# A fused attention and two-layer block kernel: one of its products computed from seven block products in place of eight

## The chip, the core and the metric

The kernel runs on one core of a Trainium2 chip. The core has a tensor engine (PE, with its weight loads shown apart as PEld), a vector engine (DVE), a scalar engine (ACT), a general engine (POOL) and SP, which here issues the DMAs. SBUF is the on-chip memory; PSUM is the memory into which PE writes. The metric is the device time of one execution in microseconds (us).

## What is computed

Four batches of 576 tokens. First a masked attention with 8 heads of 64, then a mixing layer, then a gated layer:

```python
def _moe_ref(x, mu_k, mu_r, w_k, w_v, w_r):
    x_prev = np.concatenate([np.zeros((B, 1, D)), x[:, :-1, :]], axis=1)
    xk = mu_k * x + (1.0 - mu_k) * x_prev
    xr = mu_r * x + (1.0 - mu_r) * x_prev
    k = np.maximum(xk @ w_k, 0.0)             # 512 -> 1024
    v = k * k @ w_v                           # 1024 -> 512
    r = 1.0 / (1.0 + np.exp(-(xr @ w_r)))     # 512 -> 512
    return r * v
def _moe2_ref(x, w_in, w_spatial, b_spatial, w_out):
    h = np.maximum(x @ w_in, 0.0)             # 512 -> 1024
    u, v = h[..., :512], h[..., 512:]
    v_n = (v - mean(v)) / sqrt(var(v) + 1e-6)
    v_s = einsum('ts,bsd->btd', w_spatial, v_n) + b_spatial
    return (u * v_s) @ w_out
```

The product that the change touches is `xr @ w_r` of the last batch.

## The kernel before

Channels lie on partitions in blocks of 128 (the 512 channels are 4 blocks), tokens along the free dimension. The mixing layer works on a batch in two halves of 288 tokens. A matrix number is held as a high and a low part, and a product is the sum of three matmuls of 128x128 by 128x288: high by high, high by low, low by high. They add up in one PSUM bank per output block; three banks `psM` (names psM_93, psM_94, psM_102) serve these products in turn.

For each batch b and half hf, `moe1_k` (line 1472) makes k with 8 output blocks of 4 inputs, and its square with high and low parts (`sq_dt`, on ACT, DVE and POOL); `moe1_r` (line 1539) makes r with 4 output blocks of 4 inputs and writes the Tanh of each from PSUM into `xs[b]` on ACT; `moe1_v` (line 1559) makes v with 4 output blocks of 8 inputs, and a DVE instruction (`gate`, line 1567) multiplies it into `xs[b]` from PSUM, which frees the bank. After that the second layer takes `xs[b]`: vt, u (from seven block products for batches 1 to 3, `fast_u`, line 1877), sp and out. Its PSUM banks `psB` are in the room that the attention's banks had.

Weights come as pairs of 32-bit words. `split_weight` (line 646) takes one by chunks of 128x512: a load of 512 KB into one of two buffers `raw2` issued by SP, two passes on ACT (`tmp<-raw`, `raw<-raw`), one on DVE (`lower`, line 705: `tmp<-tmp,raw`) after which the buffer can be loaded again, then the high part (a cast, ACT or DVE) and the low part (a subtraction, DVE or POOL). w_in has 8 such chunks, w_out 4; w_out's high and low parts go into the room of w_r (`square_`), which must be done with. The w_spatial loads follow through the same two buffers; PE transposes them.

The two buffers and w_in's parts lie in the SBUF pool "w2", which takes the place of the attention's pool "att" at the right side of SBUF. `open_w2` (line 1669) opens it when all users of the attention's keys are done:

```python
    def open_w2(e):
        stacks["att"].close()
        enter("two", "w2", side="right", reuse_waits="tile")
    ...
    plan.at = 4905
    add({}, open_w2, w=["w2"], after=users_of(att_keys), lat=0)
```

The order of all instructions on all engines is set before the program runs: every step is put on a list (`Plan`, line 191) with its estimated time on each engine that can do it, the keys it reads and writes, and a place `plan.at`; a list scheduler takes the steps by priorities, which a table `TUNE` of numbers shifts by tag, and picks the engine. The instructions are then issued in that order through a helper (line 497, so the profile shows L497 for all), and are kept in it.

## Time and profile before

| | us |
|---|---|
| three runs | 570.43, 573.19, 573.49 |
| median | 573.19 |
| profiled execution | 570.87 |
| its span, first to last instruction | 569.1 |
| PE busy in the span | 558.2 (98%) |
| DVE, ACT, POOL busy | 361.8, 263.9, 143.3 |
| mean granted TensorE clock | 0.999 |

The profiled execution is one of its own; 1.8 us of its time lie outside the span. A name such as `psM<-xh,wk` is output and inputs; buffer numbers are left out. Idle time of an engine is put down to what ended it.

### The profile page before, as it was taken

What the parts mean: (1) busy time and instruction counts of PE and PEld (TensorE: products, weight loads), DVE (VectorE), ACT (ScalarE), POOL (GpSimd) and SP (SyncE); (2) the same over time, 40 slices, a digit from 0 to 9 for tenths busy, and PEclk for the clock granted to TensorE, in tenths of its full rate; (3) what the DMA queues carried; (4) which work ended last, traced back from release to release, by engine and by line L of the source; (5) the groups of instructions that cost most, each with busy time, mean ns of one, the idle gap of its engine ahead of it and who ended that gap; (6) DMA issues with size and microseconds to landing.
All of it is one profiled execution on the core that took longest, in us unless ns stands there. A gap on an engine that the chain in (4) does not pass through costs nothing.

```text
span 569.1 us, 13965 instructions
## 1 busy us (share of the span) xinstructions
PE 558.2 (98%) x5810; PEld 504.7 (89%) x5821; DVE 361.8 (64%) x808; ACT 263.9 (46%) x599; POOL 143.3 (25%) x159
## 2 busy tenths in 40 slices
PE   8899999999999999999999999999999999999997
PEld 5567878799999999999999999989879988998996
DVE  3789889667976485466816245575598438857740
ACT  2779874451763552568936151263253234203131
POOL 0011201450233441313112026016411712104040
PEclk9999999999999999999999999999999999999999
DMA  8999972560461041333400001300010010001002
GB/s 191 251 239 262 235 169 44 131 123 11 90 126 49 2 86 38 96 111 132 134 32 2 1 1 46 79 2 2 37 38 1 0 56 37 1 1 74 2 1 93
DMA packets 86688, 43.10 MB, mean 76 GB/s; under 512 B 71968, under 2 KB 79648, under 8 KB 86624
## 3 DMA queue, kind: packets, MB, share of 16 engines
q1 hardware_dynamic: 86624, 42.21, 30.7%
q8 instruction: 45, 0.74, 0.6%
q14 instruction: 19, 0.16, 0.1%
HBM read 37.47 MB, written 4.72 MB: 74 GB/s over the span
## 4 chain that ended last, share of the span: by engine, by line
PE 89%; SPq 4%; ACT 2%; DVE 2%; DMA 2%; issue 1%; DVEq 0%; ACTq 0%
PE psM L497 64%; PE psB L497 18%; PE psT L497 5%; SPq L497 4%; PE psS L497 2%; DMA vw<-in_v_dram 1%; DMA ld<-in_k_dram 0%; ACT xh L497 0%; DVE temps L497 0%; DVE st L497 0%; DVE xm L497 0%; ACT vw L497 0%; DVE wk L497 0%; ACT tmp L497 0%; ACT room L497 0%
## 5 line engine op out<-in xcount | busy, mean ns | idle before, releaser
L497 PE MATMUL psM<-sq_dt.float32r,wv 128*128 128x288 f32 (+2 forms) x768 | 113.0, 297 | 0.4 <-ACT x L497 0.2
L497 PEld LDWEIGHTS psM<-sq_dt.float32r,wv 128*128 128x128 f32 x768 | 104.6, 188 | 2.4 <-ACT x L497 0.9
L497 PE MATMUL psM<-xh,wk 128*128 128x288 f32 (+2 forms) x320 | 92.7, 341 | 0.0
L497 PE MATMUL psM<-xh,square 128*128 128x288 f32 (+2 forms) x256 | 64.4, 309 | 0.6 <-ACT kr L497 0.6
L497 PEld LDWEIGHTS psM<-xh,wk 128*128 128x128 f32 x320 | 58.4, 188 | 5.2 <-DVE pr L497 0.5
L497 PE MATMUL psM<-xh,lasting 128*128 128x288 f32 x192 | 57.8, 301 | 0.0
L497 PE MATMUL psM<-xl,lasting 128*128 128x288 f32 x192 | 56.4, 294 | 0.0
L497 ACT ACTIVATE kr<-psM 128x288 f32<-128x288 f32 (+2 forms) x59 | 24.1, 411 | 57.7 <-PE psM L497 54.4
L497 PEld LDWEIGHTS psM<-xh,square 128*128 128x128 f32 x256 | 44.5, 188 | 2.6 <-ACT kr L497 1.6
L497 PE MATMUL psB<-wi,lasting 128*128 128x512 f32 x176 | 45.6, 395 | 0.0
L497 POOL TENSOR_TENSOR sq_dt.float32r<-kr,sq_dt.float32r 128x288 fp32r<-128x288 f32 (+2 forms) x29 | 24.3, 839 | 64.7 <-DVE sq_dt.float32r L497 51.0
L497 PE MATMUL psB<-square,gh 128*128 128x512 f32 (+1 forms) x136 | 40.4, 381 | 0.0
L497 PEld LDWEIGHTS psB<-wi,lasting 128*128 128x128 f32 x176 | 32.3, 188 | 6.9
L497 PE MATMUL psM<-wsh,vh 128*128 128x288 f32 x128 | 38.1, 298 | 0.0
L497 PE MATMUL psM<-xl,square 128*128 128x288 f32 (+2 forms) x128 | 37.9, 296 | 0.0
L497 PE MATMUL psM<-wsh,vl 128*128 128x288 f32 x128 | 37.8, 295 | 0.0
L497 PE MATMUL psM<-wsl,vh 128*128 128x288 f32 x128 | 37.8, 295 | 0.0
L497 PEld LDWEIGHTS psM<-xh,lasting 128*128 128x128 f32 x192 | 36.0, 188 | 0.6 <-DVE x L497 0.2
L497 PEld LDWEIGHTS psM<-xl,lasting 128*128 128x128 f32 x192 | 36.0, 188 | 0.0
L497 DVE CAST sq_dt.float32r<-kr 128x288 fp32r<-128x288 f32 (+2 forms) x38 | 11.8, 310 | 37.2 <-ACT kr L497 37.2
L497 DVE SCALAR_TENSOR_TENSOR xm<-x,mu,xm 128x288 f32<-128x288 f32 (+2 forms) x56 | 30.5, 557 | 7.0 <-ACT xm L497 6.5
L497 DVE TENSOR_TENSOR g<-psM,bb 128x288 f32<-128x288 f32 x32 | 14.5, 456 | 31.7 <-PE psM L497 25.1
(199 smaller groups left out, 1237.3 us busy)
## 6 DMA issues: line engine op xcount, KB each, us to landing
vw<-in_v_dram SPq DMA_DIRECT2D x36, 128.0 KB, 3.1
room<-in_moe_w_k_dram SPq DMA_DIRECT2D x8, 512.0 KB, 9.0
room<-in_moe_w_v_dram SPq DMA_DIRECT2D x8, 512.0 KB, 7.6
raw<-in_moe_w_in_dram SPq DMA_DIRECT2D x8, 512.0 KB, 3.9
vw<-in_v_dram SPq DMA_DIRECT2D x8, 288.0 KB, 5.8
ld<-in_q_dram SPq DMA_DIRECT2D x32, 72.0 KB, 2.7
ld<-in_k_dram SPq DMA_DIRECT2D x32, 72.0 KB, 2.6
room<-in_moe_w_r_dram SPq DMA_DIRECT2D x4, 512.0 KB, 5.7
```

The costliest lines, as they stand in the source:

```text
L497: return self.tc.keep_in_program_order(getattr(self.engine, name)(*args, **kw))
```

## The change

r of batch 3 (both halves at once) is no longer made by `moe1_r`. The matrix product is cut in blocks: the 512 inputs into two halves, the 512 outputs into two halves, the 576 tokens into two halves. Eight block products make it in the plain way; here seven do (Strassen, in Winograd's form), on sums of weight blocks (`sumh`, `suml`) and of token blocks (`tokh`, `tokl`). `open_rs` closes the attention's pool, opens a pool "rs" in its place, and makes the weight sums; `moe1_r7` mixes the tokens into `mixed`, makes their parts and sums, and adds the seven products up in place in `mixed` (2 copies and 14 additions); `moe1_r7_gate` writes the Tanh of each into `xs[3]`. The pool "w2" now takes the place of "rs", so `open_w2` waits for all steps of these functions. All numbers in `TUNE` are replaced, which changes the order and the choice of engines in many places.

```diff
--- before.py
+++ after.py
 TUNE = {
...
-    ('r', 3, 0): {'g': (5327, -33735, 792, 22), 'psM': (-6229, -150948, 792, 22), 'xh': (-8333, 200588, 200, 22), 'xl': (-5995, 87640, 0, 300), 'xm': (-5709, 229219, 792, 22)},
-    ('r', 3, 1): {'g': (-5636, -92591, 792, 22), 'psM': (-4640, 98437, 792, 22), 'xh': (-5279, -52865, 792, 22), 'xl': (-5431, -79038, -600, 0), 'xm': (-7328, -219772, 400, 22)},
+    ('r7', 3): {'g': (-7563, -43040, 792, 22), 'psM': (-6469, 1566, 792, 22), 'rc': (1719, -9997, 792, 22)},
+    ('rT', 3): {'rTh': (-2631, 10737, 792, 22), 'rTl': (-8567, 5537, 0, 300), 'rmix': (-1886, 16678, -200, -300), 'rpart': (-7239, -787, -600, -800)},
+    ('rs sums',): {'rS': (-4347, -9753, 1500, 2000), 'rst': (-6149, 34735, -600, 2000), 'rsy': (72, -12010, -600, 22)},
...
+    SEVEN = (3,)
+    QW = DM // 2
+    rs_ops = set()
+    def rs(shape, dtype, name):
+        return lambda: get("rs", shape, dtype, name)
+    mixed_all = rs([P, NC, S], F32, "mixed")
...
+    made_keys = set()
+    def open_rs():
+        att_keys = [
+            key for key in plan.written
+            if key == "mask" or isinstance(key, tuple)
+            and key[0] in ("ld", "vw", "qT", "kT", "pr", "mx", "sm", "pt", "psS", "psT")
+        ]
+        def emit(e):
+            stacks["att"].close()
+            enter("rs", "rs", side="right", reuse_waits="tile")
+            enter("two", "psB", space=PSUM, reuse_waits="tile")
+        plan.at = 4900
+        plan.tag = ("rs room",)
+        add({}, emit, w=["rs"], after=users_of(att_keys), lat=0)
...
+        for j in range(2):
+            plan.at = 5000 + 20 * j
+            parts = []
+            for y in range(2):
+                o = lambda y=y: flat()[:, y * CH : (y + 1) * CH]
+                key = ("wr", j + 2 * y, 0)
+                add(
+                    {"pool": pool(CH), "dve": dve(CH)},
+                    lambda e, o=o, key=key: two(e, o(), f32(chunk(key, 0)), f32(chunk(key, 1)), ALU.add),
+                    r=["rs", (key, 0), (key, 1)], w=[("rsy", y)], two=True,
+                )
+                parts.append([lambda o=o, z=z: o()[:, z * QW : (z + 1) * QW] for z in range(2)])
...
+            for i, x, y, op in (
+                (0, a21, a22, ALU.add), (1, lo[0], a11, ALU.subtract), (2, a11, a21, ALU.subtract),
+                (3, a12, lo[1], ALU.subtract),
+            ):
...
+                add(
+                    {"pool": pool(QW), "dve": dve(QW)},
+                    lambda e, i=i, x=x, y=y, op=op, lo=lo: two(e, lo[i](), x(), y(), op),
+                    r=[("rsy", 0), ("rsy", 1)] + dep, w=[("rst", i)], two=True,
+                )
...
+            add(
+                {"act": act(4 * QW), "dve": dve2(4 * QW)},
+                lambda e, j=j, st=st: copy(e, sum_h()[:, j], st()),
+                r=los, w=[("rS", j, 0)], two="both",
+            )
+            add(
+                {"pool": pool(4 * QW), "dve": dve(4 * QW)},
+                lambda e, j=j, st=st: two(e, sum_l()[:, j], st(), f32(sum_h()[:, j]), ALU.subtract),
+                r=los + [("rS", j, 0)], w=[("rS", j, 1)], two=True,
+            )
...
+    def product7(m, ps, key, wof, xof):
+        for j in range(2):
+            def emit(e, j=j):
+                wh, wl = wof[0](j, m)
+                rh, rl = xof[0](j)
+                o_ = ps[:, :HALF]
+                nc.tensor.matmul(o_, wh, rh, start=j == 0, stop=False)
+                nc.tensor.matmul(o_, wh, rl, start=False, stop=False)
+                nc.tensor.matmul(o_, wl, rh, start=False, stop=j == 1)
+            add(
+                {"pe": pe(3, HALF)}, emit,
+                r=wof[1](j) + xof[1](j) + ([key] if j else []), w=[key], lat=200 if j else 0,
+            )
+    def moe1_r7(b, base):
+        plan.at = base
+        plan.tag = ("rm", b)
...
+        for c in range(NC):
+            mk = ("rmix", c)
+            made_keys.add(mk)
+            def before_(e, c=c):
...
+            add(
+                {"act": act(S), "dve": dve2(S)}, before_,
+                r=["rs", ("rest", 1), *xkeys(b, 0, c)], w=[mk], two="both", after=free,
+            )
+            add(
+                {"dve": 130 + S * 1.042},
+                lambda e, c=c: nc.vector.scalar_tensor_tensor(
+                    mixed_all()[:, c], xs[b][:, c, 1 : 1 + S], mu[:, 1, c : c + 1], mixed_all()[:, c],
+                    op0=ALU.mult, op1=ALU.add,
+                ),
+                r=[mk, ("mu", 1), *xkeys(b, 0, c)], w=[mk], two=True,
+            )
...
+        plan.tag = ("rT", b)
...
+        for i, o, p, q_, dep in (
+            (0, t0, lambda: x(0, 1), lambda: x(0, 0), []),
+            (2, t2_, lambda: x(1, 1), lambda: x(0, 1), []),
+            (1, t0, lambda: x(1, 1), t0, []),
+            (3, t0, lambda: x(1, 0), t0, []),
+        ):
...
+            add(
+                {"pool": pool(2 * HALF), "dve": dve(2 * HALF)},
+                lambda e, o=o, p=p, q_=q_: two(e, o(), p(), q_(), ALU.subtract),
+                r=own + ([tk] if i in (1, 3) else []), w=[tk], two=True, after=before_t2,
+            )
+            add(
+                {"act": act(2 * HALF), "dve": dve2(2 * HALF)},
+                lambda e, i=i, o=o: copy(e, tok_h()[:, i], o()), r=[tk], w=[("rTh", i)], two="both",
+            )
+            add(
+                {"pool": pool(2 * HALF), "dve": dve(2 * HALF)},
+                lambda e, i=i, o=o: two(e, tok_l()[:, i], o(), f32(tok_h()[:, i]), ALU.subtract),
+                r=[tk, ("rTh", i)], w=[("rTl", i)], two=True,
+            )
+        plan.tag = ("r7", b)
+        gone = users_of(own + [("rmix", "t2")])
...
+        for m in range(2):
+            def place(ff, th, m=m):
+                return lambda: mixed_all()[:, 2 * ff + m, th * HALF : (th + 1) * HALF]
...
+            plan.at = base + 100 + 100 * m
+            pa, ka = bank()
+            product7(m, pa, ka, W(0, 0), X[0, 0])
+            add(
+                {"act": actp(HALF), "dve": dve(HALF)},
+                lambda e, ps=pa, o=place(1, 0): copy(e, o(), ps[:, :HALF]),
+                r=[ka], w=[key_of(1, 0)], after=gone,
+            )
+            for w, x_, adds in (
+                (W(2, 0), X[1, 0], [((0, 0), (1, 0))]),
+                (SW(1), TX(1), [((0, 1), (1, 0))]),
+                (SW(2), TX(2), [((1, 1), (0, 1))]),
+                (W(2, 1), TX(3), [((1, 0), (1, 1))]),
+                (SW(0), TX(0), [((1, 1), (1, 1)), ((0, 1), (0, 1))]),
+                (SW(3), X[1, 1], [((0, 1), (0, 1))]),
+            ):
+                plan.at += 15
+                ps, key = bank()
+                product7(m, ps, key, w, x_)
+                for o, i in adds:
+                    add(
+                        {"dve": dve(HALF)},
+                        lambda e, o=place(*o), i=place(*i), ps=ps: two(e, o(), ps[:, :HALF], i(), ALU.add),
+                        r=[key, key_of(*i)], w=[key_of(*o)], after=gone,
+                    )
...
+    def moe1_r7_gate(b, hf):
+        plan.tag = ("r7", b)
+        for o in range(NC):
+            users = set()
+            for xk in xkeys(b, 1, o):
+                users |= plan.read[xk]
+            add(
+                {"act": act(HALF)},
+                lambda e, o=o: nc.scalar.activation(
+                    xs[b][:, o, hf * HALF : (hf + 1) * HALF],
+                    mixed_all()[:, o, hf * HALF : (hf + 1) * HALF], AF.Tanh, scale=0.5,
+                ),
+                r=[("rc", o, hf)], w=[("g", b, o, hf)], table="exp", after=users,
+            )
...
+        if b == min(SEVEN):
+            n0 = len(plan.ops)
+            open_rs()
+            rs_ops.update(range(n0, len(plan.ops)))
         for hf in range(2):
             base = 1000 * (2 * b + hf + 1)
             plan.at = base
             kk = moe1_k(b, hf)
             plan.at = base + r_at[2 * b + hf]
-            moe1_r(b, hf)
+            if b in SEVEN:
+                n0 = len(plan.ops)
+                if hf == 0:
+                    moe1_r7(b, plan.at)
+                plan.at = base + r_at[2 * b + hf]
+                moe1_r7_gate(b, hf)
+                rs_ops.update(range(n0, len(plan.ops)))
+            else:
+                moe1_r(b, hf)
...
-    att_keys = [
-        key for key in plan.written
-        if key == "mask" or isinstance(key, tuple) and key[0] in ("ld", "vw", "qT", "kT", "pr", "mx", "sm", "pt", "psS", "psT")
-    ]
-
     def open_w2(e):
-        stacks["att"].close()
+        stacks["rs"].close()
         enter("two", "w2", side="right", reuse_waits="tile")
-        enter("two", "psB", space=PSUM, reuse_waits="tile")
 
...
     plan.at = 4905
     plan.tag = ("p2",)
-    add({}, open_w2, w=["w2"], after=users_of(att_keys), lat=0)
+    add({}, open_w2, w=["w2"], after=set(rs_ops), lat=0)
```

On PE, the end of r(3,0) in before and of r in after. `xh,square` and `xl,square` are tokens by w_r, `sumh` and `suml` weight sums, `wv` is v. Before:

```order
L497 MATMUL psM_94<-xh_1_887,square 128x288
L497 MATMUL psM_94<-xh_1_914,square 128x288
L497 MATMUL psM_94<-xl_928,square 128x288
L497 MATMUL psM_94<-xh_1_914,square 128x288
L497 MATMUL psM_102<-sq_dt.float32r,wv_0_0_945 128x288 x2
L497 MATMUL psM_102<-sq_dt.float32r,wv_0_1_952 128x288
L497 MATMUL psM_93<-sq_dt.float32r,wv_0_0_1064 128x288 x2
L497 MATMUL psM_93<-sq_dt.float32r,wv_0_1_1075 128x288
```

After:

```order
L500 MATMUL psM_93<-xh_1_1647,sumh 128x288
L500 MATMUL psM_93<-xl_1663,sumh 128x288
L500 MATMUL psM_93<-xh_1_1647,suml 128x288
L500 MATMUL psM_94<-sq_dt.float32r,wv_0_0_946 128x288 x2
L500 MATMUL psM_94<-sq_dt.float32r,wv_0_1_951 128x288
L500 MATMUL psM_102<-sq_dt.float32r,wv_0_0_946 128x288 x2
L500 MATMUL psM_102<-sq_dt.float32r,wv_0_1_951 128x288
L500 MATMUL psM_93<-sq_dt.float32r,wv_0_0_946 128x288 x2
```

In before the outputs of r stand among those of v; in after the seven products stand in a row, 84 matmuls, and v(3,0) begins behind them.

On DVE, the end of batch 3: the gates of v(3,1) (`x<-x,psM`) and the passes of the last weight chunks (`tmp<-tmp,raw` is `lower`, `square` holds w_out's parts, `tmp<-wi,wi` adds two planes of w_in for the u product). Before:

```order
L497 TENSOR_TENSOR sq_dt.float32r<-kr_664,sq_dt.float32r 128x288
L497 SCALAR_TENSOR_TENSOR x_1297<-x_1297,psM_94 128x288
L497 CAST square<-tmp_0_3679 128x512
L497 CAST square<-tmp_1_3652 128x512
L497 SCALAR_TENSOR_TENSOR x_1297<-x_1297,psM_102 128x288
L497 SCALAR_TENSOR_TENSOR tmp_0_3679<-tmp_0_3679,raw_0_3609 128x512
L497 CAST square<-tmp_0_3679 128x512
L497 SCALAR_TENSOR_TENSOR tmp_1_3652<-tmp_1_3652,raw_1_3596 128x512
L497 TENSOR_TENSOR tmp_0_3679<-wi_0_0_3701,wi_0_1_3716 128x512
L497 SCALAR_TENSOR_TENSOR x_1297<-x_1297,psM_93 128x288
L497 TENSOR_TENSOR tmp_1_3652<-wi_0_0_3782,wi_0_1_3792 128x512
L497 SCALAR_TENSOR_TENSOR x_1297<-x_1297,psM_94 128x288
```

After:

```order
L500 SCALAR_TENSOR_TENSOR x_1297<-x_1297,psM_94 128x288
L500 SCALAR_TENSOR_TENSOR x_1297<-x_1297,psM_102 128x288
L500 SCALAR_TENSOR_TENSOR x_1297<-x_1297,psM_93 128x288
L500 SCALAR_TENSOR_TENSOR tmp_1_4391<-tmp_1_4391,raw_1_4350 128x512
L500 CAST square<-tmp_1_4391 128x512
L500 TENSOR_TENSOR square<-tmp_1_4391,square 128x512
L500 TENSOR_TENSOR tmp_1_4391<-wi_0_0_4516,wi_0_1_4526 128x512
L500 SCALAR_TENSOR_TENSOR tmp_0_4410<-tmp_0_4410,raw_0_4361 128x512
L500 CAST square<-tmp_0_4410 128x512
L500 TENSOR_TENSOR square<-tmp_0_4410,square 128x512
L500 TENSOR_TENSOR tmp_0_4410<-wi_0_0_4438,wi_0_1_4445 128x512
L500 SCALAR_TENSOR_TENSOR x_1297<-x_1297,psM_94 128x288
```

In before two `lower` passes stand between the gates; in after two chunks with `lower`, cast and subtraction, and an addition each, stand ahead of the last gate.

On DVE in the middle of batch 3, where the products are added up in `mixed` (`psM` first is the PSUM bank, `xm` a mix for k). Only after has these rows:

```order
L500 TENSOR_TENSOR sq_dt.float32r<-kr_678,sq_dt.float32r 128x288
L500 TENSOR_TENSOR mixed<-psM_102,mixed 128x288
L500 TENSOR_TENSOR mixed<-psM_93,mixed 128x288
L500 TENSOR_TENSOR mixed<-psM_94,mixed 128x288 x2
L500 TENSOR_TENSOR mixed<-psM_102,mixed 128x288
L500 TENSOR_TENSOR mixed<-psM_94,mixed 128x288
L500 SCALAR_TENSOR_TENSOR xm_540<-x_1297,mu,xm_540 128x288
L500 TENSOR_TENSOR mixed<-psM_102,mixed 128x288
L500 SCALAR_TENSOR_TENSOR xm_542<-x_1297,mu,xm_542 128x288
```

They stand in the place where before had mixes and casts for r(3,0) and r(3,1).

## Rows read from the trace of the kernel before

**Rows 1.** The page, parts 1 and 4: busy time by engine; the chain.

```profile
PE 558.2 (98%) x5810; PEld 504.7 (89%) x5821; DVE 361.8 (64%) x808; ACT 263.9 (46%) x599; POOL 143.3 (25%) x159
...
PE 89%; SPq 4%; ACT 2%; DVE 2%; DMA 2%; issue 1%; DVEq 0%; ACTq 0%
```

**Rows 2.** Waits of PE from 150 to 569 us: total, times, longest.

```profile
PE psM L497 <- DVE gl L497: 0.3, 1, 0.3
PE psM L497 <- ACT u L497: 0.2, 1, 0.2
PE psM L497 <- ACT x L497: 0.2, 1, 0.2
```

**Rows 3.** Table by stretches: busy us (count) per engine, PEclk, DMA share, GB/s.

```profile
30.00:60.00 30.00, 29.09 (x440) 22.30 (x430) 27.69 (x75) 25.78 (x62) 7.46 (x9) 1.00 1.06 243
60.00:90.00 30.00, 28.73 (x427) 22.96 (x432) 26.59 (x56) 22.05 (x50) 0.83 (x4) 1.00 0.76 178
241.80:288.00 46.20, 46.02 (x345) 45.62 (x345) 31.59 (x71) 34.22 (x75) 10.58 (x8) 1.00 0.39 126
288.00:345.00 57.00, 57.00 (x432) 57.00 (x431) 24.45 (x58) 23.43 (x58) 12.99 (x15) 1.00 0.00 1
300.00:330.00 30.00, 30.00 (x228) 30.00 (x227) 15.11 (x36) 12.11 (x29) 3.64 (x4) 1.00 0.01 1
```

**Rows 4.** Tile xh, 299 to 312 us: min/median/max ns, first and last start.

```profile
L497 PE MATMUL psM<-xh,square x32: 291/295/330, 300.7 to 310.6; 128*128 128x288 f32 x32
```

**Rows 5.** DVE's groups, 424 to 436 us: busy us, mean ns | idle before.

```profile
L497 DVE TENSOR_TENSOR u<-psM,u 128x288 f32<-128x288 f32 x14 | 6.1, 452 | 0.6 <-PE psM L497 0.5
...
L497 DVE TENSOR_TENSOR vl<-vt,vh 128x512 fp32r<-128x512 f32 x2 | 1.4, 682 | 0.0
```

**Rows 6.** DVE's groups, 390 to 430 us.

```profile
L497 DVE TENSOR_TENSOR sums<-u,sums 128x1024 fp32r<-128x1024 f32 x2 | 2.4, 1221 | 0.0
...
L497 DVE TENSOR_TENSOR gl<-u,gh 128x576 fp32r<-128x576 f32 x3 | 2.2, 749 | 0.0
```

**Rows 7.** SP's timeline around 251, 252, 280 and 283 us: start, duration.

```profile
251.47 0.93 SPq L497 DMA_DIRECT2D raw<-in_moe_w_in_dram  x2
...
252.07 0.33 SPq L497 DMA_DIRECT2D raw<-in_moe_w_in_dram  x1
...
280.06 0.33 SPq L497 DMA_DIRECT2D raw<-in_moe_w_out_dram  x1
...
283.14 0.33 SPq L497 DMA_DIRECT2D raw<-in_moe_w_out_dram  x1
```

**Rows 8.** Tile raw (the two load buffers), 240 to 290 us.

```profile
L497 ACT ACTIVATE raw<-raw x12: 659/666/687, 248.4 to 286.8; 128x512 uint32<-128x512 uint32 x12
L497 ACT ACTIVATE tmp<-raw x10: 655/669/680, 247.9 to 280.9; 128x512 f32<-128x512 f32 x10
L497 DVE SCALAR_TENSOR_TENSOR tmp<-tmp,raw x10: 676/684/696, 250.8 to 282.4; 128x512 uint32<-128x512 uint32 x10
...
DMA to landing us min/median/max: 3.6/3.7/5.1
```

**Rows 9.** ACT's groups, 288 to 345 us (this one is the Tanh).

```profile
L497 ACT ACTIVATE x<-psM 128x288 f32<-128x288 f32 x7 | 2.9, 411 | 5.7 <-PE psM L497 5.7
```

**Rows 10.** DVE's groups, 288 to 345 us.

```profile
L497 DVE TENSOR_TENSOR sq_dt.float32r<-kr,sq_dt.float32r 128x288 fp32r<-128x288 f32 x8 | 3.7, 465 | 0.7 <-ACT sq_dt.float32r L497 0.5
L497 DVE SCALAR_TENSOR_TENSOR x<-x,psM 128x288 f32<-128x288 f32 x7 | 3.2, 455 | 13.6 <-PE psM L497 13.6
```

**Rows 11.** DVE's groups, 241 to 287 us.

```profile
L497 DVE TENSOR_TENSOR sq_dt.float32r<-kr,sq_dt.float32r 128x288 fp32r<-128x288 f32 x8 | 4.7, 594 | 5.0 <-ACT sq_dt.float32r L497 4.9
```

**Rows 12.** Timelines of DVE and of POOL, 338 to 352 us.

```profile
343.08 0.42 DVE L497 CAST square<-tmp 128x512 fp32r<-128x512 f32 x1
343.78 1.44 DVE L497 CAST square<-tmp 128x512 fp32r<-128x512 f32 x1 [0.28 <-PE psM L497]
...
343.65 1.29 POOL L497 TENSOR_TENSOR square<-tmp,square 128x512 fp32r<-128x512 f32 x1 [1.21 <-DVE square L497]
```

113 lines of the change are left out of this document (90 added, 23 removed), and 212 rows, old and new, of the table TUNE.

## The prediction

> **What bounds the kernel now.** I read the page first: the tensor engine PE is busy 558.2 of 569.1 us, and the chain that ended last lies on PE for 89% of the span [rows 1]. The other engines have room (DVE 64%, ACT 46%, POOL 25%). Then the waits of PE: from 150 us to the end there are three, of 0.3, 0.2 and 0.2 us [rows 2]. Then a table by stretches: from 241.8 to 288 and from 288 to 345, the two stretches that the change touches, PE is busy 46.02 of 46.20 and 57.00 of 57.00 us at a granted clock of 1.00, which is the 2.4 GHz level [rows 3]. So here a matmul less is time less, and any delay that makes PE wait is time more. Before 90 us PE has gaps: 0.91 us in 30 to 60 and 1.27 us in 60 to 90 [rows 3].
>
> **The level.** The profiled execution took 570.87 us. The three runs lie at 570.43, 573.19 and 573.49, so their median is 2.3 us above it. The sum is made against 570.87; of the four times the mean is 572.0, and the forecast is put on that.
>
> **Part 1, the products.** r of batch 3 is 4 outputs x 4 inputs x 3 matmuls x 2 halves = 96 matmuls of 128x288 in before. The seven block products for 2 rows of output blocks, with 2 inputs and 3 matmuls each, make 84. From 300 to 330 us, which is such work alone, 228 matmuls take 30.00 us [rows 3], 131.6 ns each. Their weight loads are 100% beside them and go with them. 12 x 0.1316 = **-1.58 us**. Nothing else in the change shortens PE's list.
>
> **Part 2, the seven products' own additions.** A plain r needs one Tanh per output. The seven products leave PSUM through 2 copies on ACT and 14 additions on DVE, into `mixed` in SBUF. An addition of that form and size takes 452 ns [rows 5]: 14 x 0.452 = 6.3 us on DVE, under 84 x 0.1316 = 11.05 us of PE. Six of seven products have one addition or two, a product holds one of three PSUM banks, and PE takes 0.79 us for one. That fits, but barely where two additions follow. The nearest case is u in the last stage, which is seven products already: one of the waits of rows 2 (0.2, for ACT u) stands there. I take **+0.2 us**, bounds 0 and 0.5.
>
> **Part 3, preparing them.** The sums of weights and tokens are new work of DVE, ACT and POOL. Rows for such shapes: 1221 ns for a 128x1024 subtraction, 749 ns for a 128x576 one [rows 6]. Weights: 2 x (2 x 0.68 + 4 x 0.40 + 1.22) = 8.4 us (0.68 from the 128x512 row of rows 5; 0.40 my estimate for half of it with the same start cost); tokens: 8 x 0.75 = 6.0 us. All on DVE that would be 14.4 us. From 241.8, where the attention's room is free, to about 303, where the products begin, DVE has 14.6 us idle in the first stretch and some 9 of the second's 32.5 [rows 3], and the weight loads of part 4 leave this place (12 x 0.68 = 8.2 us of DVE). I cost it at **0**; without that cover (DVE already full there), PE would wait for the last token sum, up to 1 us. The bounds are 0 and 1.0.
>
> **Part 4, the weight loads that are moved.** This is the term that decides. In before, w_in (8 loads of 512 KB) and w_out (4) go into two `raw2` buffers as soon as the attention's room is free: SP issues them from 251.47 (the second of that group at 252.07) up to 280.06 and 283.14 [rows 7], and PE waits 0.2 us in all that time. In after the same room holds the sums, products and results of the seven products first. `open_w2` waits for all of them, the last Tanh among them, so SP's first w_in waits for that Tanh, and all twelve loads, their splits on ACT and DVE, and the w_spatial loads behind them on SP begin anew there.
>
> When: the matmuls of r(3,0) end at 310.6 + 0.3 = 310.9 in before [rows 4]. In after PE has 84 matmuls of r7 where before had 48 of r(3,0), and 9 fewer of others ahead: (84 - 48 - 9) x 0.1316 = 3.55, so r7 ends at about 314.5. Two chained additions (0.45 each, the first overlapped in part) and a Tanh of 0.41 [rows 9], with issue, give the first load at 316.0 and the second buffer's first at 316.65.
>
> How fast: each buffer repeats landing (3.7), two ACT passes (0.67 + 0.67, less overlap) and a DVE pass (0.68) [rows 8] before it can be loaded again. Back to back that is 3.7 + 0.67 + 0.56 + 0.68 + 0.1 = 5.75 us. Before's pace: (280.06 - 251.47) / 4 = 7.15 for one buffer and (283.14 - 252.07) / 4 = 7.77 for the other [rows 7], with ACT 34.22 and DVE 31.59 of 46.2 us busy [rows 3]. The work beside is now k and v of batch 3, less dense, so I take 6.8, nearer to the measured pace than to the floor.
>
> When it is done: the twelfth load is issued after five repeats, 316.65 + 5 x 6.8 = 350.65, lands at 354.35, is through ACT at 355.6 and lowered on DVE at 356.3. Behind it on DVE stand, in its program, a cast (0.42 [rows 12]), a subtraction (0.68 [rows 5]), an addition for w_spatial's planes (0.69, same size) and then the gate of v(3,1)'s last output (0.455 [rows 10]), which frees the PSUM bank that the first output of u(0) wants: 358.3. PE comes to that step 103 steps of three matmuls after r7: 314.5 + 103 x 3 x 0.1316 = 355.2. PE waits **+3.1 us** in one place or in two or three (the earlier ones, for kl of k(3,1) and for the other gates, stand behind the same DVE passes and are part of the same delay). With the floor of 5.75 the wait is nothing; with before's mean pace of 7.46 it is 3.1 + 5 x 0.66 = 6.4. In before this work was hidden by batches 2 and 3; what remains of the cover is the 40.7 us between r7 and that step.
>
> **Part 5, the order of the start.** The table of numbers is new for every stage, and some ten operations before 90 us change places. PE's gaps there between 30 and 90 us are 2.2 us; I take 0, bounds -1 and +1.
>
> **Sum**: 570.87 - 1.58 + 0.2 + 3.1 = 572.6, that is +1.7 us. On the mean level, 572.0 + 1.7 = **573.7 us**.
>
> **Rivals.** (A) As summed: 573.7. For it: the release of the loads hangs on the last Tanh, as the program states, and the repeats are bounded by rows on both sides.
>
> (B) The loads run at before's pace, and it is slower: PE waits 6.4 us, 570.87 - 1.58 + 0.2 + 6.4 = 575.9, on the mean level 577.0. It decides from a pace of about 7.05 us, where the wait passes 4.25 us. For it: it is the only pace that the trace shows, and DVE now takes the low parts of w_in as well, which POOL took (8 x 0.68 = 5.4 us in the stretch). Against: k and v have fewer operations beside than batch 2 with two mixes.
>
> (C) The loads run near the floor and there is no wait: 570.87 - 1.58 + 0.2 = 569.5, on the mean level 570.6. Then the change does just what its arithmetic says, and 1.4 us is inside 0.5%. For it: ACT is busy 23.43 and DVE 24.45 of 57 us in 288 to 345 [rows 3].
>
> (D) A shared port. At 343.08 a DVE cast of 128x512 took 0.42 us; at 343.78 the same cast took 1.44, while POOL's subtraction ran from 343.65 to 344.94 [rows 12]: it ended 0.28 us after POOL did. The square's subtraction took 594 ns beside POOL's w_in work and 465 after it [rows 11, 10]. In after POOL has none of this work, so DVE loses no time to it: 8 x 0.129 = 1.0 us on the passes that were hit, and the pace would come to about 6.6: 573.7 - 1.0 = 572.6. The Trainium skill, page "SBUF — State Buffer", section "Who interferes with whom", says that a DVE instruction with two SBUF inputs contends with a GpSimd instruction that reads SBUF, and that the loser is blocked fully; by that rule the low parts belong on one engine. The trace agrees (1.44 against 0.42).
>
> (E) The new order closes PE's gaps in the start: 2.2 us less, and with no wait for the loads, 569.5 - 2.2 = 567.3, on the mean level 568.4. Against: the chain there runs through loads whose bytes do not change.
>
> **How the numbers follow.** A 0.40, B 0.28, C 0.12, D 0.12, E 0.08. 0.5% is 2.87 us, about what a measurement of this kernel can tell from no change. Faster by more: E, 0.08. Within: A, C and D, 0.64. Slower by more: B, 0.28. The range reaches from C with the start's lower bound, 570.6 - 1.0 = 569.6, to B with part of the start's upper bound, 577.8; outside it lie E and the far end of B.
>
> **What would show it.** Right: in the changed kernel SP's first w_in load is issued near 316 us, its releaser ACT; DVE's lowering is the main releaser of the later ones; PE waits 1.5 to 4 us in total between 340 and 362 us, for DVE's x (gates) or sq (kl); within r7 it waits less than 0.5; the granted clock stays 1.00. Wrong: no PE wait there (C), over 4.2 (B), PE waiting ahead of r7 for token or weight sums (part 3), or a stretch of the start that moves by over 1 us. The forecast also fails if w_spatial's transposes, last in SP's queue, come later than the u and vt products can cover, which no row of before prices.

## The result, and the profile after

The changed kernel took 575.04 us (median of ten runs, 573.04 to 578.99), the kernel before beside it 570.54 (ten runs, 569.57 to 573.49): ratio 1.0076, interval 1.0048 to 1.0104. It is slower by 0.76%, some 4.3 us, although PE has 12 matmuls less. Its profiled execution took 574.56 us with a span of 572.7, against 570.87 and 569.1 before: 3.69 us to account for.

The page, parts 1 and 4, as [rows 1]: busy us by engine, then the chain that ended last.

```profile
PE 557.9 (97%) x5809; PEld 502.3 (88%) x5809; DVE 391.1 (68%) x855; ACT 266.4 (47%) x593; POOL 132.6 (23%) x150
...
PE 87%; DVE 5%; ACT 2%; SPq 2%; DMA 2%; issue 1%; DVEq 0%; ACTq 0%
```

DVE has 29 us more work, and its share of the chain goes from 2% to 5%. The waits of PE from 150 us to the end, as [rows 2], total, times, longest:

```profile
PE psM L500 <- DVE sq_dt.float32r L500: 2.4, 1, 2.4
PE psM L500 <- DVE x L500: 1.2, 2, 0.8
PE psM L500 <- DVE zero L500: 0.6, 1, 0.6
PE psM L500 <- DVE u L500: 0.6, 1, 0.6
PE psM L500 <- DVE gl L500: 0.2, 1, 0.2
PE psM L500 <- DVE kr L500: 0.2, 1, 0.2
```

Three short waits have become seven, 5.2 us in place of 0.7. The table by stretches, as [rows 3], with one stretch more:

```profile
30.00:60.00 30.00, 29.70 (x444) 22.75 (x445) 28.31 (x78) 26.02 (x62) 6.00 (x7) 1.00 1.11 250
60.00:90.00 30.00, 28.82 (x460) 23.29 (x461) 27.12 (x60) 21.67 (x47) 0.84 (x4) 1.00 0.90 176
241.80:288.00 46.20, 45.79 (x344) 45.43 (x344) 32.98 (x61) 26.73 (x61) 12.11 (x13) 1.00 0.00 1
288.00:345.00 57.00, 56.82 (x428) 56.54 (x427) 38.54 (x87) 30.20 (x66) 4.78 (x6) 1.00 0.26 84
345.00:362.00 17.00, 13.13 (x94) 12.20 (x93) 15.23 (x27) 7.55 (x16) 5.20 (x6) 1.00 0.50 149
```

The same last stretch of the kernel before:

```profile
345.00:362.00 17.00, 17.00 (x130) 16.76 (x129) 8.80 (x18) 4.52 (x10) 7.04 (x6) 1.00 0.37 93
```

From 345 to 362 us PE was never idle before; now it is idle for 3.87 us, and DVE, which had 8.80 us of work there, has 15.23 of 17. At 131.6 ns each the 94 matmuls are 12.37 us of work, so 17.00 - 12.37 = **4.63 us** are lost: 3.87 of idle time and 0.76 beside it. Some 0.5 of the 0.76 is how the rows count: the row of one matmul is 0.295 us long [rows 4] while the next one starts 0.1316 after it, so the last one ahead of each of the three stops counts 0.16 us of waiting as busy. The other 0.27 has no row of its own; missing records can make it. PE's timeline there shows the stops, in brackets the idle time ahead and what ended it:

```profile
345.80 1.61 PE L500 MATMUL psM<-sq_dt.float32r,wv 128*128 128x288 f32 x11
349.82 2.79 PE L500 MATMUL psM<-sq_dt.float32r,wv 128*128 128x288 f32 x17 [2.41 <-DVE sq_dt.float32r L500]
353.45 0.66 PE L500 MATMUL psM<-sq_dt.float32r,wv 128*128 128x288 f32 x3 [0.83 <-DVE x L500]
...
359.88 0.80 PE L500 MATMUL psM<-lasting,wi 128*128 128x288 f32 x4 [0.62 <-DVE zero L500]
```

PE waits for the low part of a square of k(3,1), for a gate of v(3,1), and for the last gate, whose PSUM bank a product of u of batch 0, u(0), wants (a tiny step, `zero`, stands right behind that gate). What DVE does in the meantime, in its timeline:

```profile
347.26 0.80 DVE L500 SCALAR_TENSOR_TENSOR tmp<-tmp,raw 128x512 uint32<-128x512 uint32 x1 [0.30 <-ACT tmp L500]
348.10 0.80 DVE L500 CAST square<-tmp 128x512 fp32r<-128x512 f32 x1
348.82 0.94 DVE L500 TENSOR_TENSOR sq_dt.float32r<-kr,sq_dt.float32r 128x288 fp32r<-128x288 f32 x1
349.69 1.18 DVE L500 TENSOR_TENSOR square<-tmp,square 128x512 fp32r<-128x512 f32 x1
...
356.85 0.69 DVE L500 SCALAR_TENSOR_TENSOR tmp<-tmp,raw 128x512 uint32<-128x512 uint32 x1 [0.21 <-ACT tmp L500]
357.58 0.43 DVE L500 CAST square<-tmp 128x512 fp32r<-128x512 f32 x1
358.04 0.69 DVE L500 TENSOR_TENSOR square<-tmp,square 128x512 fp32r<-128x512 f32 x1
358.76 0.69 DVE L500 TENSOR_TENSOR tmp<-wi,wi 128x512 f32<-128x512 f32 x1
359.38 0.45 DVE L500 SCALAR_TENSOR_TENSOR x<-x,psM 128x288 f32<-128x288 f32 x1
```

The lowering, cast and subtraction of chunks of w_out (`tmp<-tmp,raw`, `square<-tmp`, `square<-tmp,square`) stand in DVE's program ahead of the square's low part and of the gates. Each engine's order is fixed, so PE waits behind work whose result it doesn't need yet. The chain that ended last goes the same way: from PE at 341 through ACT and DVE passes, one landing, and DVE to PE at 359.88:

```profile
341.39 0.41 ACT kr L500
...
347.26 0.81 DVE tmp L500
...
351.87 3.63 DMA raw<-in_moe_w_out_dram
...
356.85 0.70 DVE tmp L500
...
359.46 0.36 DVE x L500
...
359.88 1.87 PE psM L500 x12
```

And SP's timeline, as [rows 7], start and duration of each group of loads:

```profile
315.75 22.67 SPq L500 DMA_DIRECT2D raw<-in_moe_w_in_dram  x8
340.75 11.45 SPq L500 DMA_DIRECT2D raw<-in_moe_w_out_dram  x4
```

The first load is issued at 315.75, the twelfth at 351.87. The kernel before, in the same view:

```profile
233.38 35.11 SPq L497 DMA_DIRECT2D raw<-in_moe_w_in_dram  x8
```

Its first two loads go out at 233.38 and 241.77. The group at 251.47 in [rows 7], which the prediction takes for the first loads, is the third and fourth, so the start moved by 82 us and not by 64. Before's pace of 7.15 and 7.77 us holds, since it is counted from the third load on.

### The profile page after: what moved, and what is told of

Read it like the earlier page. It is cut to its first block, busy times and chain, and to the rows that moved or that the text cites. A ratio compares the mean times of both kernels' runs of the same rounds, so it can differ in the third digit from the quotient of the medians.

```text
span 572.7 us, 13973 instructions
## 1 busy us (share of the span) xinstructions
PE 557.9 (97%) x5809; PEld 502.3 (88%) x5809; DVE 391.1 (68%) x855; ACT 266.4 (47%) x593; POOL 132.6 (23%) x150
## 4 chain that ended last, share of the span: by engine, by line
PE 87%; DVE 5%; ACT 2%; SPq 2%; DMA 2%; issue 1%; DVEq 0%; ACTq 0%
PE psM L500 61%; PE psB L500 16%; PE psT L500 7%; PE psS L500 3%; SPq L500 2%; DMA early<-in_q_dram 1%; DMA raw<-in_moe_w_out_dram 1%; DVE square L500 1%; DVE mixed L500 1%; DVE gl L500 0%; DVE tmp L500 0%; DVE xm L500 0%; DVE u L500 0%; ACT raw L500 0%; ACT tmp L500 0%
## 5 line engine op out<-in xcount | busy, mean ns | idle before, releaser
L500 PE MATMUL psM<-xh,square 128*128 128x288 f32 (+2 forms) x208 | 52.8, 312 | 0.4 <-ACT kr L500 0.4
L500 POOL TENSOR_TENSOR xl<-xm,xh 128x288 fp32r<-128x288 f32 (+1 forms) x25 | 21.7, 879 | 87.8 <-ACT xh L500 75.9
L500 PEld LDWEIGHTS psM<-xh,square 128*128 128x128 f32 x208 | 36.1, 188 | 2.0 <-ACT kr L500 1.0
L500 ACT ACTIVATE kr<-psM 128x288 f32<-128x288 f32 (+2 forms) x49 | 20.1, 412 | 32.5 <-PE psM L500 31.5
L500 POOL TENSOR_TENSOR sq_dt.float32r<-kr,sq_dt.float32r 128x288 fp32r<-128x288 f32 (+1 forms) x27 | 23.1, 858 | 50.1 <-DVE sq_dt.float32r L500 32.8
L500 PE MATMUL psM<-xl,square 128*128 128x288 f32 (+2 forms) x104 | 30.8, 296 | 0.0
L500 DVE SCALAR_TENSOR_TENSOR xm<-x,mu,xm 128x288 f32<-128x288 f32 (+2 forms) x48 | 26.7, 564 | 4.2 <-ACT xm L500 3.6
```

The source lines that it names most:

```text
L500: return self.tc.keep_in_program_order(getattr(self.engine, name)(*args, **kw))
```

## The experiments

Medians in us; the ratio is to the kernel before, run beside. "Numbers" are those of the table `TUNE`, which set the order. Five theories were in play, numbered as in the expectations: (1) the start of the loads, 82 us later, sets the end; (2) the seven products' own work on DVE and ACT costs the time, or DVE is full in that stretch whatever the start; (3) DVE's passes are long because POOL reads SBUF beside them; (4) the weight chunks' passes on DVE and ACT, now among k(3,1) and v(3,1), are too much work ahead of the last gate, wherever PE stops; and, without a number there, (5) one badly placed stop costs it, and another order at that stop mends it.

**Twelve matmuls less in the kernel before.**

```diff
-                nc.tensor.matmul(ps[:, :cols], llo, rhi, start=False, stop=j == n - 1)
+                if j not in short:
+                    nc.tensor.matmul(ps[:, :cols], llo, rhi, start=False, stop=j == n - 1)
...
+            product(n, ps, key, weight_terms("wr", cs, xx, b), b == 0 and "wr" in WHOLE, (1, 2) if b == 3 and o < 3 else ())
```

> The kernel before, in its own order, without 12 of the 96 matmuls of r(3) (low part of w_r by high part of the tokens, for inputs 1 and 2 of outputs 0 to 2), so r(3) is not the reference's to the last bits. This is what the seven products take away from PE, and nothing else. Expected by all theories: 12 x 0.1316 = 1.6 us less, 0.9972 of before. A rival (PE is not the bound there, or its waits grow by what it saves): no change.

Measured: 569.15, ratio 0.9968 (0.9945 to 0.9991), that is -1.8 us (-3.1 to -0.5). The gain that the seven products bring on PE is real and of the size worked out; it is lost elsewhere.

**The kernel before with its loads held.**

```diff
...
-    add({}, open_w2, w=["w2"], after=users_of(att_keys), lat=0)
+    held = [i for i in range(k_first, len(plan.ops)) if plan.ops[i][-1][0][0] == "kr"][0]
+    add({}, open_w2, w=["w2"], after=users_of(att_keys) | {held}, lat=0)
```

> The kernel before, with one thing added: the opening of the pool for the load buffers also waits for the first relu of k(3,1) (about 320.5 us in the trace of before, 4.8 us later than the first load of after). r(3) is plain; the order is planned anew with the numbers of before. Theory 1 (the twelve loads moved behind batch 3's r cost the time): the loads take 36 us as in after, so the last is issued at about 357, its gate is free at 364 to 365 where PE comes at 357, and w_spatial follows later still; PE waits 7 to 15 us in total between 350 and 400 us, and the time is 8 to 15 us over before. Theory 2 (the work of the seven products on DVE and ACT costs the time, the loads do not): no r7 here, so before plus 0 to 1 us.

Measured: 586.45, ratio 1.0254 (1.0213 to 1.0294), 15.5 us over before, just past the 8 to 15 of theory 1. The first two loads still go out at 234.35 and 242.74, as before's do; what the edit holds back is their passes, and with them the other ten loads, from 331.92 to 363.25. Late loads can cost 15 us, but in another way than in the changed kernel: here the w_spatial loads, last in SP's queue, begin only at 366.40, and PE waits for them. The two longest of its waits from 300 to 400 us:

```profile
PE psB L497 <- DMA raw<-in_moe_w_spatial_dram: 5.1, 2, 2.9
PE psB L497 <- DVE wsl L497: 2.8, 2, 1.7
```

The changed kernel has neither wait, so this run shows the danger and not the cause. At the gates it speaks against theory 1: its twelfth load is issued 11 us later than the changed kernel's, and yet PE is busy 16.45 of the 17 us from 345 to 362, since the last gate (357.73) doesn't stand behind that load's passes there.

**The two buffers in the changed kernel, free early.** They get a pool of their own beside the seven products' room, together with the buffers `tmp2` that the passes write; the order is the changed kernel's.

```diff
...
+            enter("two", "wl", side="right", reuse_waits="tile")
             enter("rs", "rs", side="right", reuse_waits="tile")
...
-            tiles["raw2", i] = pools["w2"].tile([P, 2 * CH], U32, tag=f"raw2_{i}", name=f"raw2_{i}")
+            tiles["raw2", i] = pools["wl"].tile([P, 2 * CH], U32, tag=f"raw2_{i}", name=f"raw2_{i}")
...
```

> The kernel after, in its own order; only the two load buffers and the two number buffers get a pool of their own that opens with the pool of the seven products. To make room the low parts of the token and weight sums overwrite the high parts, so the values of r(3) are not the reference's. The first two loads are then issued in batch 2; their ACT passes stand where they stood, behind the last Tanh. Theory 1 (chain of the loads): ACT's first pass starts at about 315.7 in place of 319.6, the twelfth load is issued 3 to 4 us sooner (about 348.2 against 351.9), PE's waits of 345 to 360 us fall from 3.9 to 0.5 to 1.5 us, and the time falls by 3 to 4.5 us, to about before's or 1 us under it. Theory 2 (the seven products' own work, or DVE being full in that stretch whatever the start): waits stay at 3 us or more and the time falls by less than 1 us.

Measured: 574.10, ratio 1.0048 (1.0028 to 1.0069), 1 us under the changed kernel by the medians and 1.6 by the ratios, whose intervals overlap; theory 1 expected 3 to 4.5. The first load is issued at 231.72 in place of 315.75, but the last at nearly the same time (SP's timeline, then the table by stretches):

```profile
231.72 106.50 SPq L500 DMA_DIRECT2D raw<-in_moe_w_in_dram  x8
340.58 11.41 SPq L500 DMA_DIRECT2D raw<-in_moe_w_out_dram  x4
...
345.00:362.00 17.00, 13.01 (x94) 12.09 (x92) 15.03 (x27) 7.42 (x16) 5.00 (x6) 1.00 0.48 149
```

ACT's passes still stand behind the last Tanh, so the early landing lets the first of them start at 315.42 in place of 319.55, 4.1 us sooner. Of that the third load keeps 1.5 us (320.04 in place of 321.52) and the sixth 0.2 (331.14 in place of 331.35): each further load waits for a pass whose place in ACT's and DVE's programs has not moved. PE is still idle for 3.99 us in the stretch, as theory 2 expected of a DVE that is full whatever the start. With the order kept, theory 1 falls.

**POOL without its subtractions.** The seven low parts of batch 0 that POOL makes are filled by a memset instead.

```diff
...
-            lambda e: two(e, lo(), src(), f32(hi()), ALU.subtract),
+            lambda e: nc.gpsimd.memset(f32(lo()), 0.0) if fill and e == "pool" else two(e, lo(), src(), f32(hi()), ALU.subtract),
...
```

> The kernel after, in its own order; the seven low parts of batch 0 that POOL makes at 343.4 to 350.3 us by a subtraction are filled by a memset (writes alone, no reads), so u(0) and vt(0) are not the reference's. In after DVE's two-input passes beside them took 0.80 to 1.29 us where the same forms take 0.43 to 0.69. Theory 3 (the port that DVE and POOL share for reads makes part of the delay): those passes fall to 0.43 to 0.70 us, 2.8 us in sum, PE's waits in 345 to 360 us fall from 3.9 to 1.2 to 2 us, and the time by 2 to 2.8 us. Theory 1 alone (start of the loads and their landing): DVE waits for ACT or for a landing in any case, and the time falls by under 0.7 us.

Measured: 574.24, ratio 1.0052 (1.0029 to 1.0074). DVE's passes became short (its timeline; in the changed kernel the same cast and subtraction took 0.80 and 1.18):

```profile
347.87 0.43 DVE L500 CAST square<-tmp 128x512 fp32r<-128x512 f32 x1
348.21 0.45 DVE L500 TENSOR_TENSOR sq_dt.float32r<-kr,sq_dt.float32r 128x288 fp32r<-128x288 f32 x1
348.58 0.68 DVE L500 TENSOR_TENSOR square<-tmp,square 128x512 fp32r<-128x512 f32 x1
```

So the long passes do come from POOL's subtractions, which ran from 343.40 to 350.32 in the changed kernel. (The Trainium skill, "SBUF — State Buffer", "Who interferes with whom", says that a DVE instruction with two SBUF inputs contends with a GpSimd instruction that reads SBUF. GpSimd is POOL; the two subtractions agree, 0.45 and 0.68 in place of 0.94 and 1.18. The cast has one input, and was longer too.) That it is POOL's reads, this run doesn't show: its memsets are over by 344.0, so POOL stands idle beside these passes. The time fell by 0.8 us (1.4 by the ratios), not by 2 to 2.8. PE does 102 matmuls in the 17 us in place of 94, and the last gate ends at 358.75 in place of 359.83: POOL's part in theory 3 is true and worth about 1 us. The passes are as many, and the twelfth load still comes at 350.34.

**Another order at the first stop.** The last two low parts of the square go ahead of the first w_out chunk's passes on DVE; the rest of the order is kept.

```diff
...
-    for i, e in plan.order():
+    for i, e in kept(plan.order(), set(chunk_), first):
```

> The kernel after with two instructions of DVE moved: the low parts of the last two squares of k(3,1) stand ahead of the first w_out chunk's lowering, cast and subtraction, not between and behind them. PE's stop of 2.4 us at 347 us waits for the first of the two. If that stop sets the time, it goes, and the time falls by 1.5 to 2.4 us. If the last gate sets it (it stands behind the twelfth load's passes, and DVE has as much to do before it as in after), PE stops there for as much longer: the sum of the waits in 345 to 362 us stays within 0.8 us of 3.9 and the time within 0.5 us of after. I expect the second.

Measured: 575.46, ratio 1.0081 (1.0059 to 1.0103): as slow as the changed kernel run beside it (575.62). PE's timeline:

```profile
348.69 2.50 PE L500 MATMUL psM<-sq_dt.float32r,wv 128*128 128x288 f32 x17 [0.47 <-DVE sq_dt.float32r L500]
354.38 0.67 PE L500 MATMUL psM<-sq_dt.float32r,wv 128*128 128x288 f32 x3 [3.19 <-DVE x L500]
...
361.48 0.80 PE L500 MATMUL psM<-lasting,wi 128*128 128x288 f32 x4 [1.29 <-DVE zero L500]
```

The stop of 2.41 fell to 0.47, and those at the gates grew from 0.83 and 0.62 to 3.19 and 1.29, 4.95 us in all, a little over the 4.7 that was allowed for. Theory 5 falls: a stop that goes comes back at the next step on DVE.

**Without the passes of w_out.** Its loads stay, and the order stays.

```diff
-                lambda e, number=number, words=words: nc.scalar.activation(
+                lambda e, number=number, words=words: name != "wo" and nc.scalar.activation(
...
-            lambda e: copy(e, chunk(key, 0), number()),
+            lambda e: key[0] != "wo" and copy(e, chunk(key, 0), number()),
...
```

> The kernel after, in its own order, with w_out's four loads kept but the passes that split them left out (8 on ACT, 12 on DVE), so out is not the reference's (it multiplies by what w_r left there). Theory 4 (what costs is the split work of the last chunks, which stands in the programs of ACT and DVE between k(3,1)'s squares, batch 0's parts and v(3,1)'s gates at 341 to 360 us, whatever the start of the loads): PE's waits in 345 to 362 us fall from 3.9 to under 0.8 us and the time by 3.5 to 5 us, to 0.996 to 0.999 of before; what is left is the 12 matmuls less and the waits ahead of r7. Rival (the seven products' own additions and sums cost it, or PE's restart): waits fall by less than 1.5 us and the time stays at 1.003 or more.

Measured: 570.86, ratio 0.9997 (0.9981 to 1.0012): some 4 us of the loss are gone. The stretch:

```profile
345.00:362.00 17.00, 15.97 (x119) 15.51 (x119) 10.67 (x21) 4.61 (x13) 6.18 (x7) 1.00 0.51 160
```

PE does 119 matmuls there in place of 94, and DVE has 10.67 us of work in place of 15.23. This is what theory 4 says, if not quite in full: PE is still idle 1.03 us there where under 0.8 was expected, and the median is just over the 0.999 of before that was the upper end. The seven products' own work is all still there, so theory 2 falls as far as it means that work. The run doesn't tell DVE's passes from ACT's, nor from the turn of the buffers that hangs on both; the chain above runs through all three.

**w_out split behind w_spatial.** r7 stays where the change has it; the numbers from batch 2 on were chosen anew, since the old ones have no place for this.

```diff
...
-    plan.at = 8300
-    split_weight(
-        "p2", w_out, NC, DM, "wo",
...
     dma2(packets(P, 2304), bb, b_sp.partition_broadcast(P), r=["p2"], w=["bb"])
+    plan.at = 8300
+    split_weight(
+        "p2", w_out, NC, DM, "wo",
```

> The seven products where after has them, so the first w_in load comes at about 315.5 as in after; only w_out's split is put behind w_spatial's loads, and the numbers from batch 2 on are chosen anew by the replay. Theory 4 (what stands ahead of the gates costs, not when the loads begin): the loads of w_in begin at the same time as in after, the last of them is issued at about 337, PE's waits in 340 to 365 us fall from 3.9 to under 1 us, and the time is 569.5 to 571.5, 3.5 to 5 us under after. Theory 1 (the late start costs): waits of 3 us and more, 573 or more.

Measured: 571.96, ratio 1.0012 (0.9995 to 1.0029), 3.7 us under the changed kernel run beside it (575.62), if 0.5 over the upper end of what was expected. SP's timeline and the stretch:

```profile
316.30 21.59 SPq L500 DMA_DIRECT2D raw<-in_moe_w_in_dram  x8
341.35 11.66 SPq L500 DMA_DIRECT2D raw<-in_moe_w_spatial_dram  x8
...
369.06 11.02 SPq L500 DMA_DIRECT2D raw<-in_moe_w_out_dram  x3
...
345.00:362.00 17.00, 16.33 (x125) 15.87 (x124) 9.21 (x19) 5.01 (x15) 6.08 (x8) 1.00 0.29 79
```

The loads begin half a microsecond later than in the changed kernel, and the stops are nearly gone (0.67 us idle): not the start, but the work that stands ahead of the gates. (PE's longest wait is now 0.9 us, for `vl`, after this stretch.)

**The change with the numbers of before.** Steps that before doesn't have keep the numbers of the changed kernel. One line of the table, against the changed kernel:

```diff
...
-    ('T', 1): {'gh': (-10996, 21062, -600, 22), 'gl': (-9964, -6763, 400, 22), 'u': (-11189, -46996, 400, 300)},
+    ('T', 1): {'gh': (-6268, 16556, -600, 22), 'gl': (-14014, 16940, 792, 800), 'u': (-8012, -22407, 0, 2000)},
...
```

> The seven products with the table of numbers of before (only the tags that before did not have keep the numbers of after). This is the change without its reordering. Theory 4 with the loads held (the chain of w_in, w_out and w_spatial begins at about 316 and ends wherever the order puts it): PE waits 6 to 10 us for w_spatial's transposes and what follows them between 365 and 400 us, and the time is 6 to 10 us over before, 3 to 6 over after; so the new numbers took back part of what the seven products cost. Rival (the new order is what costs; the seven products alone gain): at before or under it.

Measured: 582.76, ratio 1.0212 (1.0173 to 1.0250). That is 11.6 us over before, more than the 6 to 10 expected. The reordering had thus taken back some 7.7 us of what the seven products cost here; a good half of that lies at w_spatial, where this run waits 3.2 us for `wsl` and 0.9 for a load (6 to 10 were expected). Part of the rest is a granted clock of 0.91 from 362 to 400 us.

**r7 ahead of k(3,0), and a control.** r7 is put before the k of its batch, with the numbers from batch 2 on chosen anew; the control is the kernel before with numbers chosen in the same way (lines of the table only).

```diff
...
+            if b in SEVEN and hf == 0:
+                n0 = len(plan.ops)
+                moe1_r7(b, base - 0)
+                rs_ops.update(range(n0, len(plan.ops)))
             plan.at = base
...
-                if hf == 0:
-                    moe1_r7(b, plan.at)
```

> The seven products put ahead of k(3,0) in the code (their banks and slots come first), and the numbers from batch 2 on chosen anew by a replay of the durations in the two traces; the rest is after. r7 then ends about 13 us sooner, at about 302, the first w_in load is issued at about 303 and the twelfth at about 340. Theory 4: the split work is spread over k(3,0), v(3,0) and k(3,1), PE's waits in 340 to 365 us fall to 1 us or less, and the time is 569 to 571.5 us, 3 to 5 under after and within 0.3% of before. Rival (the seven products cost elsewhere): 573 or more.

The control:

```diff
...
-    ('u', 0): {'psM': (-8447, 136341, 792, 22), 'u': (-9759, 172590, 0, 22)},
+    ('u', 0): {'psM': (14804, 84309, 792, 300), 'u': (-4816, 8204, -200, 22)},
...
```

> The kernel before with nothing changed but the numbers from batch 2 on, chosen anew in the same way and with the same effort as for the kernel with the seven products first; it is the measure for that kernel. By the replay it is 2 to 3 us under before and equal to that kernel within 1 us. Theory 4 expects 568 to 570.5 us: PE has hardly a wait left to lose there, so the numbers can give back no more than the 1 to 2 us of its few waits. If it is 2 us or more under the kernel with the seven products first, the products are worth nothing even without the late loads.

Measured: 571.48, ratio 1.0004 (0.9986 to 1.0022), and the control 570.26, ratio 0.9984 (0.9970 to 0.9998). Where the order is made for it, an earlier start does help: the twelfth load is issued at 341.47, and the stops on the way are 1.2, 0.6 and 0.5 us. In the kernel before, choosing the numbers anew is worth 0.2% (0.02 to 0.30).

**Both**, r7 first and w_out last, with numbers chosen anew:

```diff
...
+                moe1_r7(b, base - 0)
...
-                    moe1_r7(b, plan.at)
...
     dma2(packets(P, 2304), bb, b_sp.partition_broadcast(P), r=["p2"], w=["bb"])
+    plan.at = 8300
+    split_weight(
+        "p2", w_out, NC, DM, "wo",
```

> The seven products ahead of k(3,0) as in the run with the products first, and w_out's split put behind w_spatial's loads (w_out is wanted last, by out(0) near 395 us); numbers from batch 2 on chosen anew by the replay. Theory 4: with the split work of w_out out of the stretch of the gates and the rest spread, PE's waits in 340 to 365 us are under 0.8 us, those ahead of it (r7, k(3,0)) under 0.8 us, and the time is 568.5 to 570.5 us, that is 0.4% under before at most and level with the re-numbered kernel without the products. If it stays at 571 or more, the products cost elsewhere what they save.

Measured: 570.32, ratio 0.9994 (0.9976 to 1.0011). Two waits are left from 300 to 400 us, 0.6 and 0.5 us. That is the best of the kernels with seven products, and not to be told from the kernel before, nor is it under the control (0.9984): none of them shows the 1.6 us that twelve matmuls less are worth.

**The changed kernel once more**, beside the last three, without an edit.

> The kernel after once more, unchanged, beside the three others on their chip: 574 to 575.5 us, with PE's waits in 345 to 362 us again at 3.7 to 4.1 us in the profile.

Measured: 575.62, ratio 1.0087 (1.0062 to 1.0113), as at first. Its profiled execution (578.36 us) shows the 2.4 us stop and what followed, by stretches and in PE's timeline:

```profile
350.00:355.00 5.00, 2.58 (x17) 2.12 (x16) 4.68 (x7) 2.77 (x6) 3.55 (x4) 0.97 0.49 170
355.00:360.00 5.00, 5.00 (x27) 4.73 (x27) 4.80 (x10) 2.34 (x4) 0.00 (x0) 0.69 0.49 152
```

```profile
353.15 4.72 PE L500 MATMUL psM<-sq_dt.float32r,wv 128*128 128x288 f32 x20 [2.40 <-DVE sq_dt.float32r L500]
...
363.74 0.80 PE L500 MATMUL psM<-lasting,wi 128*128 128x288 f32 x4 [0.55 <-DVE zero L500]
```

From 355 to 360 us PE was never idle and did 27 matmuls, at a granted clock of 0.69; 5 us at 131.6 ns are 38. Little of these 1.4 us reaches the time. When the stop ended this execution was 3.33 us behind the first one (353.15 against 349.82; from 60 to 90 us its granted clock reads 0.94), and at the step of u(0) behind the last gate it was 3.86 behind (363.74 against 359.88). PE, slowed, came to the gates when they were free, and the wait of 0.83 us is not there. So the lower clock cost about 0.5 us, and the waits from 345 to 362 us are 2.4, not the 3.7 to 4.1 expected.

The stretch from 345 to 362 us in one table, from the same view of each kernel:

| kernel | PE busy | DVE busy | ratio |
|---|---|---|---|
| before | 17.00 | 8.80 | 1 |
| before, loads held | 16.45 | 8.38 | 1.0254 |
| both | 16.45 | 5.59 | 0.9994 |
| w_out last | 16.33 | 9.21 | 1.0012 |
| no w_out passes | 15.97 | 10.67 | 0.9997 |
| r7 first | 15.78 | 11.35 | 1.0004 |
| old numbers | 16.13 | 13.74 | 1.0212 |
| the change again | 14.58 | 15.90 | 1.0087 |
| POOL without subtractions | 13.84 | 13.48 | 1.0052 |
| the change | 13.13 | 15.23 | 1.0076 |
| buffers early | 13.01 | 15.03 | 1.0048 |
| another order | 12.05 | 15.80 | 1.0081 |

Of the kernels with seven products, those with under 12 us of DVE work in these 17 us keep PE busy for 15.78 or more; those with over 13 leave it at 14.6 or less, but for one. With the numbers of before, DVE has 13.74 us there and PE still 16.13: in that order the last lowering on DVE starts at 362.12, behind the last gate (358.81). So a full DVE alone doesn't stop PE; what counts is which of its work stands ahead of the step that PE wants.

## Why the prediction was right and wrong

The time, 575.04, lies in the range and on the side of the forecast, but it is the case slower by over 0.5% that came, which had 0.28, and not the likeliest. In the traces the change was to cost 1.7 us (570.87 to 572.6) and cost 3.69. That the time still came near the forecast is in part luck with the level: the mean of four, 572.0, stood 1.5 us over what before's ten runs gave. Put on that, the forecast would have been 572.2, 2.8 us under the measured time.

- **Part 1**, -1.58: right, by the run with twelve matmuls less (-1.8, within -3.1 to -0.5).
- **Part 2**, +0.2: the size is right. The 14 additions took 456 ns in the median, v(3,0) began behind r7 at 314.59 (314.5 was forecast for r7's end), and PE's only stop from 288 to 345 us is 0.2. It is not for an addition, though: it is for `kr`, a relu of k that DVE makes from a PSUM bank.
- **Part 3**, 0: 0.2 instead. From 241.8 to 288 us PE is idle for 0.41 us in place of 0.18, inside the bounds; its one stop there is 0.4 us, for a gate's `x`. DVE did not fill up as feared: 32.98 of 46.20.
- **Part 4**, +3.1: the place, the chain and the engines were right. PE would have come to that step of u(0) at 359.88 - 4.63 = 355.25 (355.2 was forecast), and the step that let it on was the last gate, behind a lowering, a cast, a subtraction and an addition on DVE, as listed. The size was 4.63. That gate ended at 359.83 in place of 358.3: the twelfth load was issued at 351.87 and not at 350.65, so the second buffer's five repeats (its first load was at 316.40) took 7.09 us each where 6.8 was taken, and what follows took 0.3 more. (The floor's sum comes to 5.71, not 5.75; nothing hangs on that.)
- **The failed step** is that pace: 6.8 us was too small by 0.29, five times, and it was taken for a free-running repeat, first load plus five times a constant. The buffers freed early show that the first load doesn't set it: it moved by 84 us, ACT's first pass by 4.1, and the twelfth load by 0.2, to 351.66. The pace is what the order of ACT's and DVE's programs allows, in which these passes alternate with those of k(3,1) that PE feeds; the runs with w_out's passes left out or moved show that it is those passes ahead of the gates that cost. DVE's share of 345 to 362 us was never added up in the prediction: 8.80 us of before, less 1.8 for the passes of w_out that are among them, plus 7.2 for four chunks of 1.8 (0.68, 0.43 and 0.69) come to 14 of 17 us.
- **Part 5**, 0: -0.6. In the first 90 us PE was busy 83.97 us in place of 83.38, inside the bounds.
- **After 362 us**, not in the sum: waits of 0.8 us, of which 0.6 for `u`, in place of 0.5, +0.3.

These come to -1.58 + 0.2 + 0.2 + 4.63 - 0.6 + 0.3 = 3.15 of 3.69. Another 0.1 lies outside the span (1.86 us in place of 1.77); for the other 0.4 I have no row.

Most of the signs named for the forecast came: the first load near 316, released by ACT; 0.2 us of waiting within r7; 3.87 us of idle time, for the squares and the gates, inside 1.5 to 4; a clock of 1.00 in the profiled execution.

The rivals: what came lies between A and B. The idle time is inside A's; the pace (7.09 against 7.05) and the time lost (4.63 against 4.25) are just past the point where B decides, and its price of 6.4 did not come. D expected DVE to be freed of POOL; instead POOL's low parts of batch 0, not of w_in, were beside DVE's passes and cost about 1 us. Its pair of 0.42 and 1.44 is also a cast, with one SBUF input, and so not a case of the rule quoted behind it; the square's subtraction (465 and 594 ns), with two, is. C and E fell: there was a wait, and the start gave 0.6, not 2.2. The condition on w_spatial was the right one to name (two runs failed by it), and the changed kernel met it.

Left open: the changed kernel with nothing but its numbers chosen anew was not run, so a part of what the run with w_out last won (0.2% by the control) can be that. The same holds for the run with r7 first.

## What to carry to other kernels

When a change takes the room in which a later stage was being prepared, add up the busy time of every engine in the stretch into which that preparation is moved, not only the pace of its loads: an engine near full there can stop the tensor engine, at whichever wanted step stands behind the work, and a better order at one stop moves it to the next. An eighth fewer matmuls in one product was worth 1.6 us on the tensor engine; finding room for the work that it displaced decided the result. Experiments that leave a block of work out, with the order kept, told the cause in one run; earlier data, or another place for one step, only ruled rivals out.
